# Block linear attention and a gated MLP on one core: the attention state moved ahead, the layer norm split over two engines, and a new order of the instructions

## The chip, the cores and the metric

The kernel runs on one core of a Trainium2 chip. The metric is device microseconds of one execution. Thirteen executions of the kernel before took 151.11 to 153.46 us, median 151.86 us.

## What is computed

q, k and v have the shape (4, 8, 768, 64): batches, heads, positions, channels. Attention is linear with a decay lam per head, and the reference does it in blocks of 64 positions:

```python
for b in range(nb):
    intra = einsum('bhic,bhjc->bhij', qb, kb) * Dmask
    out[:, :, sl] = einsum('bhij,bhjd->bhid', intra, vb) + einsum('bhid,bhde->bhie', qb * lam_pow, kv_state)
    kv_state = lam_block * kv_state + einsum('bhsd,bhse->bhde', kb * rev_pow, vb)
```

The result x (4, 768, 512) goes through a gated MLP. w_in is 512 x 1024, w_spatial 768 x 768, w_out 512 x 512:

```python
h = maximum(x @ w_in, 0.0); u, v = h[..., :512], h[..., 512:]
v_n = (v - mean(v)) / sqrt(var(v) + 1e-06)
v_s = einsum('ts,bsd->btd', w_spatial, v_n) + b_spatial
out = (u * v_s) @ w_out
```

All inputs and the output are float32; the matrix products run in bf16.

## The kernel before, in words

The 4 x 768 positions are cut into 12 tiles n of 256 positions, three for each batch. A tile is worked on in two chunks c of 128 positions. The decay is put into factors of q and v (lq, lqn, lv), so that the recurrence over blocks becomes a running sum: the state of a batch is a sum of k-transposed times v that stays in PSUM bank 7 for the three tiles and is copied to SBUF (s_sb) after each chunk.

**Who sets the order.** Nothing is scheduled by a compiler. A long string ORDER holds one token for each step, and the loop at L501 calls one helper for each token, so that each engine's queue holds its steps in the order of the string. Semaphore waits are put in from what each instruction reads and writes. A token is NAME.arguments.engine; the engines are T (TensorE, PE in the profile), D (VectorE, DVE), A (ScalarE, ACT), P (GpSimd, POOL) and S (SyncE, SP). The first argument is the tile n, or for the MLP's last steps the batch; the last is mostly the PSUM bank.

The steps of a tile, in the order in which data passes through them:

- LK, LQ, LV (`load`, L181): a DMA of 512 KB of k, q or v, asked on SP; three buffers each.
- KC, QC (`split`): a cast to bf16. TK, TQ (L300): eight 128x128 transposes on PE. EK: the copy of the transposed k to SBUF. EQ (L313): the same for q, times lq. For tiles 8 to 11 QM (L277, a product with lqn) and DMA transposes on SP (DK, DQ) take the place of QC, TK, TQ, EK and EQ.
- VD (L292): v times lv, 128 x 1024.
- SC (L329): scores, 16 matmuls of 64x64 tiles. There are two SC for each tile. MK (L333): the scores times the causal mask, on DVE.
- KV (L345): k-transposed times v onto the state in bank 7. SS (L350, a `copy`, L166): the state to SBUF.
- AV (L366 state times q, L375 scores times v): the output products of the attention, in two parts (0 and 1) for the two chunks. Both parts write the same two banks; a 64-row half of the array writes one bank in part 0 and the other in part 1.
- EX: the attention output x-transposed to SBUF.
- PV (L401) and PU (L439): x times the two halves of w_in. EV, EU (L406 on ACT, L408 on DVE): relu and eviction.
- BN (L416, L417): mean and variance on DVE. RA (L421): square root on ACT. RD (L426): reciprocal on DVE. VN (L430): (v - mean) times rstd, 128 x 512, on DVE.

The steps of a batch: PW (L461, six matmuls of 128 x 384) multiplies w_spatial, GB (L466) adds the bias, GM (L472) multiplies by u, PO (L478) multiplies by w_out, EO evicts and ST stores. WT (L451) transposes w_spatial once and EW copies it to SBUF.

The weights are float32 in memory and cast to bf16 by DMAs that GpSimd issues: WI (`w_in`, L239, two halves), WS (`w_sp`, L244, two halves), WO (`w_out`, L248). Ahead of each stands a GT token (`after`, L235), a copy of one element of a q, k or v buffer: it holds POOL's queue until that tile has landed, and so sets when the weights are asked for. GT.1.1 waits for q of tile 1 (0 is k, 1 is q, 2 is v).

The matmuls of the attention (SC, KV, AV) work on 64x64 tiles, four of them in the array at once; all others use the full array.

Of the kernel before, what the change touches and what calls it, by code (L numbers as in the profile page):

```python
# [8 lines left out]
FP32 = mybir.dt.float32  # L9
# [7 lines left out]
LK.0.2.S lam.A msk.P LQ.0.2.S LK.1.2.S idn.P mkc.D LV.0.2.S LB.6.T pos.P LN.6.A LK.2.2.S LL.D KC.0.2.P LX.A  # L17
LQ.1.2.S TK.0.6.T LT.0.A QC.0.2.D LQ.2.2.S TQ.0.5.T EK.0.6.A EQ.0.5.D KC.1.2.A SC.0.0.0.T LV.1.2.S SC.0.1.2.T
LT.2.A MK.0.0.0.D TK.1.6.T VD.0.2.P EK.1.6.A MK.0.1.2.D LV.2.2.S LT.1.A AV.0.0.0.T LK.3.2.S KV.0.0.T SS.0.0.A
GT.1.1.P WI.0.P QC.1.2.D KV.0.1.T AV.0.1.0.T KC.2.2.A LQ.3.2.S GT.1.1.P WI.1.P TQ.1.6.T EX.0.1.1.A TK.2.5.T  # L20
EQ.1.6.D GT.1.2.P WS.1.P EX.0.0.0.A QC.2.2.D EK.2.5.A SC.1.0.2.T LQ.4.2.S GT.1.2.P WS.0.P SC.1.1.0.T
MK.1.0.2.D TQ.2.6.T SS.0.1.A VD.1.2.P EQ.2.6.D MK.1.1.0.D SC.2.0.2.T SC.2.1.4.T MK.2.0.2.D AV.1.0.0.T KV.1.0.T
LV.3.2.S MK.2.1.4.D SS.1.0.A KV.1.1.T VD.2.2.P AV.1.1.0.T SS.1.1.A PV.0.0.6.T EX.1.1.1.A EX.1.0.0.A PV.0.1.1.T
EV.0.0.6.A AV.2.0.2.T BN.0.0.D PV.1.1.6.T EV.0.1.1.D KV.2.0.T BN.0.1.D PV.1.0.5.T SS.2.0.A EV.1.1.6.D RA.0.A
AV.2.1.2.T BN.1.1.D PU.1.0.6.T BS.S EV.1.0.5.A RD.0.D PU.0.1.4.T VN.0.0.D EX.2.1.3.A KC.3.2.P BN.1.0.D
EX.2.0.2.A PU.1.1.5.T EU.0.1.4.A EU.1.0.6.D PV.2.0.3.T RA.1.A VN.0.1.D EU.1.1.5.A RD.1.D TK.3.6.T VN.1.1.D
EV.2.0.3.A PU.2.0.2.T VN.1.0.D EK.3.6.A BN.2.0.D PV.2.1.3.T EU.2.0.2.A PU.2.1.6.T EV.2.1.3.A LK.4.2.S WT.3.2.T
BN.2.1.D EU.2.1.6.A QC.3.2.P WT.4.3.T WT.0.5.T EW.3.2.D RA.2.A WT.1.6.T LK.5.2.S EW.4.3.D EW.0.5.A WT.5.4.T
WT.2.2.T RD.2.D VN.2.1.D EW.5.4.A TQ.3.3.T QC.4.2.P VN.2.0.D PU.0.0.5.T EW.2.2.A EQ.3.3.D LQ.6.2.S EW.1.6.A
TQ.4.4.T VD.3.2.P SC.3.1.0.T EU.0.0.5.A EQ.4.4.D SC.3.0.2.T PW.0.0.1.6.T LQ.5.2.S MK.3.1.0.D PW.0.1.1.5.T  # L30
GB.0.0.1.6.D LV.4.2.S MK.3.0.2.D PW.0.1.0.4.T GM.0.0.1.P KC.4.2.A PW.0.0.0.6.T GB.0.1.1.5.D GB.0.1.0.4.D
LK.6.2.S GM.0.1.1.P TK.4.5.T GB.0.0.0.6.D PW.0.2.1.4.T GM.0.1.0.P EK.4.5.D LK.7.2.S AV.3.0.0.T GT.0.5.P WO.P
GB.0.2.1.4.D SC.4.0.2.T SC.4.1.5.T KV.3.0.T MK.4.0.2.D PW.0.3.1.4.T GM.0.2.1.P SS.3.0.A LV.6.2.S QC.6.2.P
MK.4.1.5.D KV.3.1.T AV.3.1.0.T KC.5.2.A PW.0.3.0.3.T GM.0.0.0.P SS.3.1.D GB.0.3.1.4.D LV.5.2.S QC.5.2.A
TK.5.6.T EX.3.1.1.D GM.0.3.1.P PW.0.2.0.2.T GB.0.3.0.3.D EX.3.0.0.A VD.4.2.P EK.5.6.A GM.0.3.0.D TQ.5.3.T
GB.0.2.0.2.D PV.3.1.5.T EQ.5.3.D PU.3.0.6.T EV.3.1.5.A GM.0.2.0.P AV.4.0.0.T BN.3.1.D EU.3.0.6.A SC.5.1.2.T
SC.5.0.4.T LQ.8.2.S KV.4.0.T MK.5.1.2.D PV.3.0.6.T SS.4.0.A MK.5.0.4.D KV.4.1.T EV.3.0.6.A AV.4.1.0.T LK.8.2.S
KC.6.2.P PO.0.0.3.T EX.4.0.0.A BN.3.0.D EX.4.1.1.A PO.0.1.6.T EO.0.0.3.D RA.3.A LK.9.2.S PV.4.0.2.T RD.3.D
SS.4.1.D EO.0.1.6.A VN.3.1.D VD.6.2.P VN.3.0.D PV.4.1.3.T EV.4.0.2.A ST.0.0.S TK.6.6.T BN.4.0.D EV.4.1.3.A
PO.0.2.2.T EK.6.6.A BN.4.1.D VD.5.2.P TQ.6.3.T LV.9.2.S EO.0.2.2.A PU.3.1.5.T EQ.6.3.D RA.4.A PO.0.3.6.T  # L40
QM.8.0.D QM.8.1.P EU.3.1.5.A ST.0.1.S RD.4.D AV.5.0.0.T VN.4.1.D EO.0.3.6.A SC.6.0.2.T VN.4.0.D SC.6.1.4.T
KV.5.0.T MK.6.0.2.D PO.0.5.6.T SS.5.0.A KC.7.2.P ST.0.3.S AV.5.1.0.T MK.6.1.4.D LQ.11.2.S TK.7.3.T EX.5.1.1.A
PU.4.0.2.T EX.5.0.0.A EK.7.3.A PV.5.1.5.T LK.10.2.S EU.4.0.2.A PV.5.0.4.T ST.0.2.S EV.5.1.5.A LQ.7.2.S
PU.5.1.3.T EO.0.5.6.A BN.5.1.D EV.5.0.4.A PO.0.4.6.T EU.5.1.3.A BN.5.0.D ST.0.5.S PU.5.0.2.T EO.0.4.6.A
LV.8.2.S RA.5.A PU.4.1.3.T EU.5.0.2.A RD.5.D VN.5.0.D AV.6.0.0.T VN.5.1.D EU.4.1.3.A KV.6.0.T ST.0.4.S
PW.1.0.0.6.T SS.6.0.A PW.1.0.1.5.T GB.1.0.0.6.D LQ.9.2.S GM.1.0.0.P PW.1.1.0.6.T GB.1.0.1.5.D LV.7.2.S
QC.7.2.D GM.1.0.1.P KV.6.1.T AV.6.1.0.T GB.1.1.0.6.D KC.8.2.A PW.1.2.0.5.T EX.6.0.0.D DQ.8.S GM.1.1.0.P
EX.6.1.1.A SS.6.1.D PW.1.2.1.6.T DK.8.S GB.1.2.0.5.D VD.8.2.P PW.1.3.0.5.T GB.1.2.1.6.D LK.11.2.S PU.6.0.6.T
GB.1.3.0.5.D GM.1.2.0.P TQ.7.4.T GM.1.3.0.D EU.6.0.6.A GM.1.2.1.P PU.6.1.5.T EQ.7.4.D LV.11.2.S QM.9.0.P
PO.1.0.6.T EU.6.1.5.A SC.7.0.0.T VD.7.2.P EO.1.0.6.A SC.7.1.2.T PO.1.2.5.T MK.7.0.0.D LQ.10.2.S PV.6.1.6.T  # L50
MK.7.1.2.D QM.9.1.P PO.1.1.4.T LV.10.2.S EV.6.1.6.A EO.1.2.5.D AV.7.0.0.T BN.6.1.D EO.1.1.4.A SC.8.1.2.T
SC.8.0.5.T KV.7.0.T MK.8.1.2.D PV.6.0.4.T ST.1.1.S SS.7.0.A KV.7.1.T MK.8.0.5.D EV.6.0.4.A AV.7.1.0.T
# [24 lines left out]
"""


@with_exitstack  # L80
def kernel(
    ctx: ExitStack,
    tc: tile.TileContext,
    q: bass.AP,
    k: bass.AP,
    v: bass.AP,
    lam: bass.AP,
    moe_w_in: bass.AP,
# [6 lines left out]
    P = 128  # L95
# [15 lines left out]
    def sb(shape, dt, name):  # L111
        return const.tile(shape, dt, name=name)
# [18 lines left out]
    lv = sb([P, NR, H, 2], FP32, "lv")  # L131
    lqn = sb([P, NR, H, 2], FP32, "lqn")
    lq = sb([P, NR, 4, 2, P], BF16, "lq")
    seen = sb([1, 1], FP32, "seen")
    eps_t = sb([P, 1], FP32, "eps_t")
    win_sb = sb([P, NCH, DFF], BF16, "win_sb")
    wout_sb = sb([P, NCH, DM], BF16, "wout_sb")
# [397 lines left out]
```

## Time and profile before

| | |
|---|---|
| Median of 13 executions | 151.86 us |
| The profiled execution | 151.52 us |
| Its span, first to last instruction | 149.7 us |
| Mean granted TensorE clock | 0.986 |
| DMA packets' data | 30.73 MB, mean 205 GB/s |

The numbers of the profile are those of the span: between span and device time lie 1.8 us. The profile page gives the busy time of each engine (PE is the matmul stream, PEld the loading of weights beside it), then the span in 40 slices of 3.74 us, where a digit is the busy share in tenths. PEclk is the clock that PE was granted. Further views are the waits (who waited for whom), the chain of work that ended last, the instructions in order of time, and tables of busy time by stretch.

### The profile page before, as it was taken

To read this page: it belongs to the slowest core of one execution; us is meant where nothing else is said; L and a number is where in the kernel's file an instruction comes from. 1 tells how busy PE (TensorE), PEld (TensorE's weight loads), DVE (VectorE), ACT (ScalarE), POOL (GpSimd) and SP (SyncE) were. 2 spreads that over 40 slices of the span, in tenths; PEclk is the share of its full clock that TensorE was granted. 3 is DMA by queue.
4 is the path that set the end of the run, shared out by engine and by line. 5 is a ranking of instruction groups with operands and counts; after the bars stand their busy time and mean duration, and the time that the engine had idled before them with its cause. 6 is when DMAs were issued, how large, how long until landed. Compare 5 with 4: busy or idle time off the path is not lost.

```text
span 149.7 us, 4756 instructions
## 1 busy us (share of the span) xinstructions
PE 135.0 (90%) x2026; PEld 88.0 (59%) x2026; DVE 106.3 (71%) x190; ACT 81.3 (54%) x146; POOL 75.2 (50%) x74
## 2 busy tenths in 40 slices
PE   1274959999999989999999999999999999999990
PEld 1263845487866754667766657557667655666540
DVE  1445492985798999994567799999949981936701
ACT  3987815398921836849812445676552245831161
POOL 7415990203739966740049967980393340016620
PEclk9999995999999999999999999999999999999998
DMA  3999999999999999999999799997170003111165
GB/s 98 299 290 290 290 216 217 216 236 309 286 278 253 217 293 283 294 309 279 333 336 198 177 307 316 107 209 262 30 120 4 2 4 140 70 70 72 70 227 198
DMA packets 52040, 30.73 MB, mean 205 GB/s; under 512 B 9522, under 2 KB 48946, under 8 KB 52018
## 3 DMA queue, kind: packets, MB, share of 16 engines
q1 hardware_dynamic: 49488, 27.53, 73.9%
q0 software_dynamic: 2384, 2.75, 10.8%
q8 instruction: 16, 0.26, 0.7%
q10 hardware_dynamic: 146, 0.13, 0.3%
q14 instruction: 6, 0.05, 0.1%
HBM read 24.77 MB, written 6.29 MB: 207 GB/s over the span
## 4 chain that ended last, share of the span: by engine, by line
PE 82%; DVE 4%; issue 2%; ACT 1%; ACTq 0%
PE ps L461 20%; PE ps L401 14%; PE ps L478 14%; PE ps L439 14%; PE ps L375 4%; PE ps L345 4%; PE ps L300 4%; PE ps L329 3%; PE ps L366 3%; DVE a_sb L333 2%; PE ps L451 1%; DVE vsb L466 1%; DVE qT L313 0%; DVE gT L472 0%; DVE o_sb L170 0%
## 5 line engine op out<-in xcount | busy, mean ns | idle before, releaser
L472 POOL TENSOR_TENSOR gT<-vsb,uT 128x384 bf16<-128x384 f32 x27 | 30.1, 1130 | 33.5 <-DVE vsb L466 33.3
L461 PE MATMUL ps<-wt_sb,vn 128*128 128x384 bf16 x192 | 33.9, 327 | 0.0
L292 POOL TENSOR_TENSOR vd<-v_in,lv 128x1024 bf16<-128x1024 f32 x12 | 22.9, 1910 | 14.4 <-issue 6.4
L333 DVE TENSOR_TENSOR a_sb<-ps,m 128x1024 bf16<-128x1024 f32 x24 | 28.4, 1214 | 1.8 <-PE ps L329 1.6
L416 DVE BATCH_NORM_STATS2 st<-vh 128x6 f32<-128x512 bf16 x24 | 16.5, 686 | 11.9 <-ACT vh L406 11.7
L461 PEld LDWEIGHTS <-vn 128*128 128x128 bf16 x192 | 17.9, 98 | 11.9
L401 PE MATMUL ps<-win_sb,xT 128*128 128x512 bf16 x96 | 24.6, 393 | 0.0
L439 PE MATMUL ps<-xT,win_sb 128*128 128x256 bf16 x192 | 24.1, 273 | 0.0
L478 PE MATMUL ps<-wout_sb,gT 128*128 128x512 bf16 x96 | 23.4, 380 | 0.0
L466 DVE TENSOR_TENSOR vsb<-ps,bsp 128x384 f32<-128x384 f32 x32 | 17.6, 552 | 6.8 <-PE ps L461 5.4
L439 PEld LDWEIGHTS <-win_sb 128*128 128x128 bf16 x192 | 18.3, 98 | 4.4
L168 ACT ACTIVATE o_sb<-ps 128x512 f32<-128x512 f32 (+1 forms) x21 | 12.4, 589 | 14.4 <-PE ps L478 10.2
L406 ACT ACTIVATE vh<-ps 128x512 bf16<-128x512 f32 x21 | 12.6, 601 | 13.5 <-PE ps L401 13.5
L406 ACT ACTIVATE uT<-ps 128x512 bf16<-128x512 f32 x22 | 13.2, 598 | 6.3 <-PE ps L439 6.1
L401 PEld LDWEIGHTS <-xT 128*128 128x128 bf16 x96 | 9.0, 101 | 9.7 <-issue 1.5
L168 ACT ACTIVATE s_sb<-ps 128x256 bf16<-128x256 f32 x14 | 5.3, 381 | 16.9 <-PE ps L345 16.9
L478 PEld LDWEIGHTS <-gT 128*128 128x128 bf16 x96 | 9.0, 98 | 8.9
L430 DVE TENSOR_SCALAR vn<-vh,mv,rstd 128x512 bf16<-128x512 bf16 x24 | 12.3, 546 | 0.3
L375 PE MATMUL ps<-a_sb,vd 64*64 64x128 bf16 x384 | 11.2, 229 | 1.1 <-DVE a_sb L333 1.1
L168 ACT ACTIVATE kc<-k_in 128x1024 bf16<-128x1024 f32 x7 | 7.4, 1056 | 7.3 <-PE ps L345 5.1
L168 ACT ACTIVATE xT<-ps 128x512 bf16<-128x512 f32 x19 | 10.5, 592 | 1.3 <-PE ps L375 1.1
L329 PE MATMUL ps<-qT,kT 64*64 64x128 bf16 x384 | 8.5, 233 | 2.3 <-DVE qT L313 2.3
(64 smaller groups left out, 156.4 us busy)
## 6 DMA issues: line engine op xcount, KB each, us to landing
k_in<-in_k_dram SPq DMA_DIRECT2D x12, 512.0 KB, 7.1
q_in<-in_q_dram SPq DMA_DIRECT2D x12, 512.0 KB, 7.4
v_in<-in_v_dram SPq DMA_DIRECT2D x12, 512.0 KB, 8.1
out_dram<-o_sb SPq DMA_DIRECT2D x23, 256.0 KB, 2.8
wsp_raw<-in_moe_w_spatial_dram POOLq DMA_DIRECT2D x2, 576.0 KB, 15.7
win_sb<-in_moe_w_in_dram POOLq DMA_DIRECT2D x2, 512.0 KB, 10.2
wout_sb<-in_moe_w_out_dram POOLq DMA_DIRECT2D x1, 512.0 KB, 8.5
bsp<-in_moe_b_spatial_dram SPq DMA_DIRECT2D x1, 384.0 KB, 8.3
```

The costliest lines, as they stand in the source:

```text
L168: nc.scalar.activation(out=o, in_=i, func=AF.Copy)
L292: vec(e).tensor_tensor(out=vd[n % NCA][:, h], in0=v_in[n % NIN][:, h], in1=lv[:, n % NR, h].unsqueeze(3).broadcast_to((P, h.stop - h.start ...
L333: nc.vector.tensor_tensor(out=a_sb[n % NA][:, i].rearrange("p o w j x -> p (o w) (j x)"), in0=bank(b, 2).rearrange("p o (w y) -> p (o w) y ...
L375: nc.tensor.matmul(out=po[row(w), c ^ o, c, i], lhsT=vd[n % NCA][row(c), 4 * o + u, j, :], rhs=a[row(c), i, o, w, j, :], start=(r == 0 and ...
L401: nc.tensor.matmul(out=bank(b), lhsT=x[:, c, g], rhs=win_sb[:, g, DH:DFF], start=(g == 0), stop=(g == NCH - 1))
L406: nc.scalar.activation(out=o, in_=i, func=AF.Relu)
L416: nc.vector.bn_stats(out=st6[p2][:, t], in_=vh[p2][:, t])
L439: nc.tensor.matmul(out=pu[:, f2].rearrange("p (c x) -> p c x", c=2), lhsT=win_sb[:, g, f * P:(f + 1) * P], rhs=x[:, :, g, :], start=(g == ...
L461: nc.tensor.matmul(out=bank(b)[:, 0:HW], lhsT=vn[bb % 2][:, s, f * P:(f + 1) * P], rhs=wt_sb[:, s, i * HW:(i + 1) * HW], start=(s == 0), s ...
L466: nc.vector.tensor_tensor(out=vsb[(bb * 4 + f) % NVS][:, i * HW:(i + 1) * HW], in0=bank(b)[:, 0:HW], in1=bsp[:, i * HW:(i + 1) * HW], op=A ...
L472: vec(e).tensor_tensor(out=gT[bb % 2][:, f, cols].rearrange("p (a y m) -> p a y m", m=2, y=Q64), in0=vsb[(bb * 4 + f) % NVS][:, cols].rear ...
L478: nc.tensor.matmul(out=bank(b), lhsT=gT[bb % 2][:, f, t * P:(t + 1) * P], rhs=wout_sb[:, f, :], start=(f == 0), stop=(f == NCH - 1))
```

## The change

The diff consists of a new ORDER and four small edits.

- State ahead: KV of the next chunk or tile now stands ahead of AV where it can (KV.1 before AV.1 is as before; KV.5.0 and KV.6.0 now stand before AV.5.0 and AV.5.1), and KV, AV and the SC of the next tile stand in one row on PE.
- Between the two parts of an AV of the tiles 3 to 11 there is a new step SY: a copy of one element of each of the two banks (ps[0:1, b:b+2, 0:1]) into `seen`, five times on ACT and four times on DVE. Part 1 writes the banks that SY reads, and SY reads what part 0 wrote, so that part 1 starts when part 0 is done.
- VN has a second form on ACT: Identity with scale rstd and bias nmr = -mean times rstd. Sixteen of the 24 VN are there. RD has one more DVE instruction, which makes nmr (128 x 2).
- The weights are asked elsewhere: WI.0 after v of tile 0, WI.1 after v of tile 1, WS.1 after k of tile 2, WS.0 after v of tile 2, WO after v of tile 5. Before: all of WI after q of tile 1, WS after q of tile 2, WO after k of tile 5.
- SP asks q, k, v of the tiles 0 to 2 as K0 Q0 V0 K1 Q1 V1 Q2 K2 V2; before as K0 Q0 K1 V0 K2 Q1 Q2 V1 V2.
- Other steps change engine: 9 instead of 3 EV, 4 instead of 2 EU and 8 instead of 5 GM are on DVE, one VD (VD.1) is on DVE, EK.0 and others go from ACT to DVE, some QC from DVE and ACT to POOL.

The work on PE is the same: 194 steps, 4051 instructions.

```diff
 ORDER = """
-LK.0.2.S lam.A msk.P LQ.0.2.S LK.1.2.S idn.P mkc.D LV.0.2.S LB.6.T pos.P LN.6.A LK.2.2.S LL.D KC.0.2.P LX.A
-LQ.1.2.S TK.0.6.T LT.0.A QC.0.2.D LQ.2.2.S TQ.0.5.T EK.0.6.A EQ.0.5.D KC.1.2.A SC.0.0.0.T LV.1.2.S SC.0.1.2.T
-LT.2.A MK.0.0.0.D TK.1.6.T VD.0.2.P EK.1.6.A MK.0.1.2.D LV.2.2.S LT.1.A AV.0.0.0.T LK.3.2.S KV.0.0.T SS.0.0.A
-GT.1.1.P WI.0.P QC.1.2.D KV.0.1.T AV.0.1.0.T KC.2.2.A LQ.3.2.S GT.1.1.P WI.1.P TQ.1.6.T EX.0.1.1.A TK.2.5.T
...
+LK.0.2.S lam.A idn.P LQ.0.2.S msk.P LV.0.2.S LK.1.2.S LB.6.T pos.P mkc.D LN.6.A LQ.1.2.S LL.D KC.0.2.P LX.A
+LV.1.2.S TK.0.6.T LT.0.A QC.0.2.D EK.0.6.D TQ.0.5.T LT.1.A LQ.2.2.S EQ.0.5.D GT.2.0.P WI.0.P LT.2.A SC.0.0.0.T
+LK.2.2.S SC.0.1.2.T VD.0.2.P MK.0.0.0.D KC.1.2.A MK.0.1.2.D LV.2.2.S TK.1.6.T AV.0.0.0.T QC.1.2.D EK.1.6.A
+KV.0.0.T TQ.1.5.T SS.0.0.D AV.0.1.0.T EQ.1.5.D KV.0.1.T EX.0.0.0.A SS.0.1.D SC.1.1.2.T SC.1.0.4.T EX.0.1.1.A
+MK.1.1.2.D LK.3.2.S MK.1.0.4.D GT.2.1.P WI.1.P PV.0.1.6.T VD.1.2.D LQ.3.2.S PV.0.0.5.T EV.0.1.6.A QC.2.2.P
+AV.1.0.0.T BN.0.1.D EV.0.0.5.A LQ.4.2.S KV.1.0.T BN.0.0.D TQ.2.6.T SS.1.0.A GT.0.2.P WS.1.P KC.2.2.A
+AV.1.1.0.T EQ.2.6.D KV.1.1.T EX.1.0.0.D SS.1.1.A TK.2.6.T EX.1.1.1.A RA.0.A PV.1.1.5.T EK.2.6.D SC.2.1.0.T
+SC.2.0.2.T EV.1.1.5.A PV.1.0.6.T MK.2.1.0.D BS.S PU.0.0.5.T RD.0.D EV.1.0.6.A BN.1.1.D GT.2.2.P WS.0.P
+VN.0.1.A PU.0.1.4.T BN.1.0.D EU.0.0.5.A VD.2.2.P PU.1.0.6.T VN.0.0.A MK.2.0.2.D EU.0.1.4.A PU.1.1.5.T RA.1.A
+EU.1.0.6.A RD.1.D VN.1.1.D AV.2.0.0.T VN.1.0.A LV.3.2.S EU.1.1.5.A KV.2.0.T SS.2.0.A KC.3.2.D AV.2.1.0.T
+EX.2.0.0.D EX.2.1.1.A TK.3.6.T PV.2.1.5.T EK.3.6.A PV.2.0.4.T EV.2.1.5.A PU.2.0.6.T BN.2.1.D EV.2.0.4.A
+LK.4.2.S WT.1.5.T BN.2.0.D EU.2.0.6.A WT.5.4.T QC.3.2.P EW.1.5.A WT.4.3.T EW.5.4.D WT.0.6.T WT.3.2.T RA.2.A
...
+SC.5.0.4.T SY.4.0.D LQ.9.2.S KV.4.1.T MK.5.1.2.D AV.4.1.0.T SS.4.1.A PV.3.1.6.T EX.4.0.0.A VD.6.2.P MK.5.0.4.D
+EX.4.1.1.A TQ.6.0.T LV.7.2.S PU.4.1.1.T EV.3.1.6.D QC.7.2.P PU.4.0.5.T EQ.6.0.D EU.4.1.1.A LV.9.2.S BN.3.1.D
+PV.4.1.6.T GT.2.5.P WO.P EU.4.0.5.D KC.6.2.A PW.0.2.1.4.T VD.5.2.P EV.4.1.6.D LK.8.2.S TK.6.5.T BN.4.1.D
+PV.3.0.6.T EK.6.5.A GB.0.2.1.4.D KV.5.0.T LV.8.2.S EV.3.0.6.D AV.5.0.0.T GM.0.2.1.P SS.5.0.A SC.6.1.2.T
+SC.6.0.4.T SY.5.0.D BN.3.0.D KV.6.0.T AV.5.1.0.T KC.7.2.P PV.4.0.6.T EX.5.0.0.A MK.6.0.4.D EX.5.1.1.A TK.7.0.T
...
-    seen = sb([1, 1], FP32, "seen")
+    seen = sb([1, 2], FP32, "seen")
...
+    nmr = many(2, [P, NT], FP32, "nmr")
...
-        nc.gpsimd.tensor_copy(out=seen, in_=(k_in, q_in, v_in)[x][n % NIN][0:1, 0, 0, 0:1])
+        nc.gpsimd.tensor_copy(out=seen[:, 0:1], in_=(k_in, q_in, v_in)[x][n % NIN][0:1, 0, 0, 0:1])
...
+    def s_y(e, n, b):
+        copy(e, seen, ps[0:1, b:b + 2, 0:1].rearrange("p z x -> p (z x)"))
...
     def r_d(e, n):
         r, p2 = n % NR, n // NR % 2
-        nc.vector.reciprocal(out=rstd[p2][:, 2 * r:2 * r + 2], in_=rstd[p2][:, 2 * r:2 * r + 2])
+        pair = slice(2 * r, 2 * r + 2)
+        nc.vector.reciprocal(out=rstd[p2][:, pair], in_=rstd[p2][:, pair])
+        nc.vector.scalar_tensor_tensor(out=nmr[p2][:, pair], in0=mv[p2][:, pair, 0], scalar=-1.0,
+                                       in1=rstd[p2][:, pair], op0=ALU.mult, op1=ALU.mult)
 
     def v_n(e, n, c):
         t, p2 = 2 * (n % NR) + c, n // NR % 2
+        if e == "A":
+            nc.scalar.activation(out=vn[p2][:, t], in_=vh[p2][:, t], func=AF.Identity,
+                                 scale=rstd[p2][:, t:t + 1], bias=nmr[p2][:, t:t + 1])
+            return
```

## The prediction

> **What bounds the kernel now.** I read the page's busy shares and slices first, then the busy time by stretch, then the PE's waits, then the chain, last the DMA queues around the weights.
>
> ```profile
> PE 135.0 (90%) x2026; PEld 88.0 (59%) x2026; DVE 106.3 (71%) x190; ACT 81.3 (54%) x146; POOL 75.2 (50%) x74
> ...
> PE   1274959999999989999999999999999999999990
> ...
> PEclk9999995999999999999999999999999999999998
> DMA  3999999999999999999999799997170003111165
> ```
>
> PE is full from the seventh slice (3.74 us each) to the last but one; it idles in the first 22 us, and in slice 7 its clock is halved. DMA is full until about 100 us.
>
> ```profile
> 22.50:36.50 14.00, 13.94 (x176) 8.75 (x175) 8.85 (x21) 9.33 (x18) 2.09 (x3) 0.88 1.17 240
> 36.50:146.10 109.60, 108.87 (x1593) 69.00 (x1592) 85.25 (x151) 56.46 (x101) 58.41 (x48) 1.00 0.79 193
> ```
>
> From 36.5 to 146.1 us (columns: length, then busy of PE, PEld, DVE, ACT, POOL, clock, DMA, GB/s) PE idles 0.73 us. So **PE's own work bounds the kernel**; only three things can be won: the start, PE time between matmuls that counts as busy, and those 0.73 us. The last 3.6 us (146.1 to 149.7: eviction and store) end with the same instructions in both kernels.
>
> ```profile
> PE ps L300 <- POOL kc L172: 2.6, 1, 2.6
> PE ps L329 <- DVE qT L313: 2.3, 3, 0.9
> PE ps L345 <- ACT s_sb L168: 1.3, 2, 0.9
> PE ps L375 <- DVE a_sb L333: 1.1, 1, 1.1
> ```
>
> After 6.1 us PE waits 5.6 us in all (the 2.6 us lie before that), 4.9 of them before 22.6 us. One stall stands later:
>
> ```profile
> 55.27 0.64 PE L329 MATMUL ps<-qT,kT 64*64 64x128 bf16 x32 [0.70 <-DVE qT L313]
> ```
>
> **Mode switches.** The chain's pieces (start, us, what) show PE time that is neither waiting nor work:
>
> ```profile
> 40.60 0.57 PE ps L329 x32
> ...
> 45.63 0.98 PE ps L461 x6
> 46.60 0.35 PE ps L375 x16
> 46.95 0.45 PE ps L329 x32
> 47.40 0.24 PE ps L345 x16
> 47.64 1.08 PE ps L461 x6
> ```
>
> 32 score matmuls (64x64 tiles) take 0.57 right after full-array transposes and 0.45 after other 64x64 work; six W_spatial matmuls (128x128) take 1.08 after 64x64 work and 0.98 after full-array work. A switch between 64x64 and full-array work costs 0.10 to 0.12, I take 0.11. Counting them in the PE order: up to the first WT 14 before and 14 after; from there on 42 before, 28 after, since SC, KV and AV now stand together ("KV.5.0 AV.5.0 SC SC KV.6.0 AV.5.1"). 14 x 0.11 = **-1.54 us**. It counts only where PE is full, as it is there; otherwise it is worth 0.
>
> **The stall at 55.27.** TQ.5 ended 2.4 us of PE work ahead of SC.5, but its qT multiply stood on DVE behind a gT product of 2.68 (L472) and an addition. Now TQ.5, PU, PU, KV, AV, SC.5: again 2.4 us, and on DVE only MK.4 stands ahead of the multiply (0.69), done by then: **-0.70**. What is late next there is counted below as new misses.
>
> **The start, step by step.** Both orders hold the same PE work before the first WT, which starts here:
>
> ```profile
> 36.53 2.20 PE L451 MATMUL ps<-ident,wsp_raw 128*64 128x128 bf16 x72
> ```
>
> So the lead of the new start is 36.5 minus its WT start. Tiles of q, k, v (512 KB) land 1.81 us apart (kc waits until 5.0, qc 6.8, kc.1 8.6, vd 10.5). The new order asks K0 Q0 V0 K1 Q1 V1 Q2 K2 V2, so V0 lands at 8.6 (was 10.5), K1 at 10.4 (was 8.6), Q1 at 12.2 (was 14.0). W_in's first half is asked when V0 is there instead of Q1. It comes through POOL's queue:
>
> ```profile
> 14.69 0.93 POOL L239 DMA_DIRECT2D win_sb<-in_moe_w_in_dram  x1
> ```
>
> Its first packets run in the 18 to 19 us stretch, some 3.7 us later, and the landing views give W_in 8.9 and 11.5 us from issue, W_spatial 14.3 and 17.1 (queued behind W_in). While POOL's transfers run, the others starve (20 to 22 us: packets, MB, share):
>
> ```profile
> q0 software_dynamic: 290, 0.29, 84.3%
> q1 hardware_dynamic: 282, 0.14, 34.9%
> ```
>
> Packets alternate one to one, and POOL's are the larger: q, k, v fall from 0.29 MB/us to 0.07. Worked on with these rates: the copy after V0 0.7, W_in half 0 issued at 9.3, flowing at 13.0, landed by 18.1; V1 lands at 15.2, Q2 18.5; W_in half 1 issued at 15.4, landed by 24.3 (26.9 with the other row); K2 at 22.1 (was about 12), W_spatial.1 issued at 22.3; V2 at 25.0, W_spatial.0 issued at 25.2, flowing behind .1, landed at **34.6** - as before (17.5 + 17.1 = 34.6).
>
> [...]
>
> PE, with the durations of its first 24 us: TK.0 6.1, TQ.0 7.5, SC.0 9.4 to 10.5 as before. K1's cast now stands behind all three LT on ACT (to 10.55), so TK.1 starts at 11.7 (was 10.4), AV.0.0 at 12.7 (12.5), KV.0.0, TQ.1 13.8 to 14.8, AV.0.1 and KV.0.1 to 16.0, SC.1 to 17.1. Then PE waits 1.0 for W_in and runs two PV (1.73, or 2.89 at half clock) that before came at 23.8. VD.1 is now on DVE behind two MK (19.1 + 1.4 = 20.5; 1.36 from two 128x512 products of L277, 1.91 from POOL), so AV.1.0 starts at 20.6; TQ.2, AV.1.1, KV.1.1 to 22.7, TK.2 waits for K2's cast to 23.2; PV.1.1 at 24.3, SC.2, PV.1.0 to 26.8, four PU to 30.3, AV.2, KV.2, a wait of 0.5 for the state copy, AV.2.1 to 32.0, TK.3, two PV, PU: **WT at 35.3**, a lead of 1.2. If the clock halves once, as here,
>
> ```profile
> 19.03:22.44 3.41, 1.78 (x77) 1.45 (x76) 3.39 (x5) 0.32 (x1) 3.06 (x2) 1.00 1.20 217
> 22.44:25.86 3.42, 3.30 (x45) 1.77 (x45) 1.08 (x1) 1.70 (x5) 0.07 (x1) 0.51 1.19 216
> ```
>
> (3.4 us with PE half busy are followed by 3.4 us at 0.51), TK.2 and PV.1.1 end about 0.8 later: lead 0.4. I take the middle, **-0.8**; bounds +0.5 (W_in half 1 and V1 both late) and -1.9 (WT can't start before 34.6).
>
> [...]
>
> **What is added.** Nine SY copies (two elements from PSUM), 5 on ACT, 4 on DVE. No row has one; 0.06 (memset 128x1) to 0.41 (128x256 from PSUM), nearest 0.18 (ACT 128x8 from PSUM, L202). PE's second AV part waits for it: 0.04 + 0.18 + 0.06 = 0.3 after the first part. Behind that wait stand all of PE's later matmuls. Cover between: for n = 4, 5, 6, 8, 9, 10 two SC and one KV (0.45 + 0.24 = 0.69), for 3, 7, 11 over 1.7. Taken at 0; without cover 0.3 each. Sixteen VN go from DVE (0.55 mean, 0.41 median) to ACT (0.60 by L406's 128x512; at least 0.30, the small sqrt); twelve 128x2 products are added on DVE (0.16 to 0.18). The same three table loads stay on ACT. With the other moves DVE carries by these rows about 3 us more and ACT 4 more, of 43 and 68 us idle: hidden behind PE; uncovered, a late VN holds up a PW on PE for as long as it is late.
>
> **New misses.** On POOL, VD.6 (1.9) waits for AV.4.1 (at 53.3), then QC.7 (1.04), the copy, the W_out issue (0.8), VD.5 (1.9): 59.2, and PE wants KV.5.0 at about 59.6; KC.7 and W_out (8.5 from issue: 65, wanted at 66) follow as tightly. Between 0 and 2.0; I take +0.4.
>
> **Sum.** Profiled execution 151.52 (span 149.7 and 1.8 around it): -0.8 - 1.54 - 0.70 + 0.40 = -2.64, 148.9. It lies 0.34 under the median of 151.86, so **149.2**.
>
> **Rivals.**
> - The start is worth all it can be: 151.86 - 1.9 - 1.54 - 0.70 = 147.7, lower if W_spatial lands early (146.8). For: WI.0 lands 5.5 us earlier. Against: K2, K1's cast and VD.1 come later. 0.15.
> - No change: no lead, POOL's chain slips 2.0: 151.86 - 1.54 - 0.70 + 2.0 = 151.6. For: margins of 0.4 there. 0.16.
> - Slower: **W_spatial lands late.** Its second half is asked at V2's landing (25.2) instead of 17.5. WT wants it at 35.7; 17.1 us as before would make 42.3, 6.6 late: 155.8; 8.5 (W_out's row) hides it. It turns the sign from a landing after 39.1, 13.9 us from issue. Against: only its own other half is ahead of it. 0.13.
> - The SY wait is bare: with two evictions (0.6 each) ahead of the copy it ends 1.5 after the first part, 0.8 uncovered, six times: 154.0; sign turns at 0.57 each. 0.06.
>
> **Chances.** The forecast, 147.9 to 151.0: 0.50. About 0.5% (0.76 us) is what a measurement tells from no change; so faster 0.65, same 0.16, slower 0.19. Range 146.8 to 152.9: it leaves out most of the slower cases and the edge of the fast one.
>
> **What would show it.** In the new profile: WT's first matmul at 34.6 to 36.1; PE idle after it under 1.2 us; half clock in one slice or none; no PE wait over 0.3 on "seen"; pieces of L461 x6 with 1.08 rarer. Wrong if WT waits for DMA, if SY shows as a releaser, or if PE idles after 40 us on POOL's vd.

## The result, and the profile after

The changed kernel took 153.8 us (median of 11 executions, 152.7 to 154.19); the kernel before, on the same chip, 152.4 us. The ratio is **1.0133, 95% interval 1.0105 to 1.016: slower by 1.3%**, where 1.8% faster was forecast. Single executions of the kernel before lie in two groups, about 151.5 and 153, and the ratios leave out a kernel's executions that are over 1.5% above its fastest, so the table below also gives the ratio of the medians over all executions (1.009 here).

The profiled execution took 154.19 us (before 151.52), its span is 152.5 us. The page, busy shares and slices (3.81 us each):

```profile
PE 135.0 (89%) x2026; PEld 87.6 (57%) x2026; DVE 109.8 (72%) x200; ACT 85.9 (56%) x158; POOL 71.9 (47%) x73
...
PE   1259598959999899999999999999999999999980
...
PEclk9999999996999999999999999999999999999998
DMA  3999999999999985999799999655674010151055
```

PE's busy time is what it was, 135.0. Its gaps, before in the fourth and sixth slices, are now in the fifth and in the ninth (5, at 30 to 34 us); in the tenth the clock falls (6). The stretches, divided at the first WT (39.58, before 36.53):

```profile
22.50:39.55 17.05, 14.63 (x228) 9.36 (x222) 10.79 (x21) 12.46 (x22) 4.82 (x6) 0.90 1.14 269
39.55:148.25 108.70, 107.67 (x1593) 69.19 (x1592) 85.42 (x158) 60.60 (x113) 57.40 (x48) 1.00 0.72 183
```

From the first WT to the last matmul it is 108.6 us (109.5 before); the start is 3.05 longer; the last eviction and store take 4.3 instead of 3.7 us (3.6 to 4.2 in the other kernels below). -0.9 + 3.05 + 0.6 = 2.8: **in this execution the start loses more than the whole.** It is the slowest of the eleven; the medians lie 1.4 us apart, not 2.8. PE's waits, in us, times, longest:

```profile
PE ps L406 <- DMA win_sb<-in_moe_w_in_dram: 1.9, 1, 1.9
...
PE ps L368 <- ACT s_sb L170: 1.4, 1, 1.4
...
PE ps L473 <- DVE vsb L478: 0.6, 1, 0.6
```

The state copy (s_sb), which the order moved ahead, is itself what PE waits for. PE's instructions around it, in order of time:

```profile
33.98 0.31 PE L368 MATMUL ps<-qT,s_sb 64*64 64x128 bf16 x8 [1.43 <-ACT s_sb L170]
...
35.19 3.50 PE L406 MATMUL ps<-win_sb,xT 128*128 128x512 bf16 x8
...
39.58 0.58 PE L463 MATMUL ps<-ident,wsp_raw 128*64 128x128 bf16 x14
```

AV.2.1 waits 1.43, and then the PV.2 pair (8 matmuls) takes 3.50, nearly twice its time in the profiles below where the clock stays (1.90). ACT's instructions show why the copy is late:

```profile
29.20 0.81 ACT L439 ACTIVATE vn<-vh,nmr,rstd 128x512 bf16<-128x512 bf16 x1 [0.82 <-DVE nmr L433]
29.92 0.57 ACT L411 ACTIVATE uT<-ps 128x512 bf16<-128x512 f32 x1
30.40 0.80 ACT L439 ACTIVATE vn<-vh,nmr,rstd 128x512 bf16<-128x512 bf16 x1
...
32.35 0.81 ACT L439 ACTIVATE vn<-vh,nmr,rstd 128x512 bf16<-128x512 bf16 x1
...
33.55 0.37 ACT L170 ACTIVATE s_sb<-ps 128x256 bf16<-128x256 f32 x1
```

Its state was complete at 32.5 (KV.2.0 ran from 32.10, 0.44). Three VN, needed by nobody before 44 us, stand ahead of it, and the first of them made ACT wait 0.82 for nmr. That product of 128x2 elements took 0.16 in eight of its twelve places, and 1.09 here, first row; the second is POOL's VD.2 beside it:

```profile
28.01 1.09 DVE L433 SCALAR_TENSOR_TENSOR nmr<-mv,rstd 128x2 f32<-128x2 f32 x1
```
```profile
27.16 1.91 POOL L294 TENSOR_TENSOR vd<-v_in,lv 128x1024 bf16<-128x1024 f32 x1
```

They end at 29.10 and 29.07. The nmr is not needed for the delay: in the run sy_four below, whose order is the same up to here, ACT did not wait for it and the copy ran at 33.55 all the same. The clock, by stretches (columns as above, the clock is the third from the end):

```profile
31.70:35.10 3.40, 1.86 (x72) 1.36 (x63) 1.90 (x6) 2.78 (x7) 0.00 (x0) 1.00 1.14 249
35.10:38.50 3.40, 3.31 (x9) 1.20 (x10) 0.99 (x3) 1.61 (x3) 0.00 (x0) 0.53 1.14 320
```

A stretch in which PE was 55% busy is followed by one at 0.53. It is the pattern that the kernel before shows once, at 19.03 to 25.86; there the first PV pair took 2.96 (23.77). Here the first pair ran slowly too (18.58, 3.40 us), but at a recorded clock of 1.00: PE's matmuls had been as slow before it (28 of SC.1 took 1.04 at 15.66; 32 of SC.2 took 0.64 at 26.14), so that no wait is shown to be the reason.

Nor does the second halving belong to the order. The run h2_rest_before below has the same order up to here, the same wait and nearly the same busy time, and its clock stays:

```profile
33.98 0.31 PE L366 MATMUL ps<-qT,s_sb 64*64 64x128 bf16 x8 [1.44 <-ACT s_sb L168]
...
35.20 1.90 PE L404 MATMUL ps<-win_sb,xT 128*128 128x512 bf16 x8
```
```profile
31.70:35.10 3.40, 1.89 (x72) 1.40 (x64) 1.89 (x6) 2.78 (x6) 0.00 (x0) 1.00 1.13 253
```

So does that of sy_four (wait 1.24 at 33.97, pair 1.90, first WT at 37.90). Of the 3.05 us that the start loses in the profile, about 1.6 are this halving, which came in one of three profiles with this wait; 1.4 are there without it.

### The profile page after: what moved, and what is told of

Its sections match the earlier page's. It is cut to its first block, busy times and chain, and to the rows that moved or that the text cites. A ratio compares the mean times of both kernels' runs of the same rounds, so it can differ in the third digit from the quotient of the medians.

```text
span 152.5 us, 4771 instructions
## 1 busy us (share of the span) xinstructions
PE 135.0 (89%) x2026; PEld 87.6 (57%) x2026; DVE 109.8 (72%) x200; ACT 85.9 (56%) x158; POOL 71.9 (47%) x73
## 4 chain that ended last, share of the span: by engine, by line
PE 64%; DVE 10%; DMA 8%; ACT 7%; SPq 6%; issue 2%; ACTq 0%; DVEq 0%
PE ps L473 20%; PE ps L406 12%; PE ps L451 11%; PE ps L490 10%; DMA k_in<-in_k_dram 8%; SPq L186 6%; DVE a_sb L335 3%; PE ps L377 2%; PE ps L331 2%; ACT vn L439 2%; DVE nmr L433 2%; PE ps L302 2%; PE ps L347 2%; DVE vsb L478 2%; PE ps L368 2%
## 5 line engine op out<-in xcount | busy, mean ns | idle before, releaser
L484 POOL TENSOR_TENSOR gT<-vsb,uT 128x384 bf16<-128x384 f32 x24 | 26.1, 1105 | 42.7 <-DVE vsb L478 41.6
L406 PE MATMUL ps<-win_sb,xT 128*128 128x512 bf16 x96 | 26.8, 419 | 2.2 <-DMA win_sb<-in_moe_w_in_dram 1.9
L294 POOL TENSOR_TENSOR vd<-v_in,lv 128x1024 bf16<-128x1024 f32 x11 | 21.0, 1905 | 10.6 <-PE ps L451 9.3
L490 PE MATMUL ps<-wout_sb,gT 128*128 128x512 bf16 x96 | 22.4, 379 | 0.0
L439 ACT ACTIVATE vn<-vh,nmr,rstd 128x512 bf16<-128x512 bf16 x16 | 12.8, 812 | 5.7 <-DVE nmr L433 5.7
L411 ACT ACTIVATE vh<-ps 128x512 bf16<-128x512 f32 x15 | 8.9, 592 | 12.7 <-PE ps L406 11.7
L170 ACT ACTIVATE xT<-ps 128x512 bf16<-128x512 f32 x21 | 11.6, 592 | 7.7 <-PE ps L377 7.7
L411 ACT ACTIVATE uT<-ps 128x512 bf16<-128x512 f32 x20 | 11.7, 590 | 5.5 <-PE ps L451 5.5
L302 PE MATMUL ps<-ident,kc 128*128 128x128 bf16 x64 | 5.8, 243 | 5.0 <-POOL kc L174 3.6
L279 POOL TENSOR_TENSOR qc<-q_in,lqn 128x512 bf16<-128x512 f32 x7 | 7.7, 1116 | 3.3 <-issue 3.3
```

The source lines that it names most:

```text
L170: nc.scalar.activation(out=o, in_=i, func=AF.Copy)
L294: vec(e).tensor_tensor(out=vd[n % NCA][:, h], in0=v_in[n % NIN][:, h], in1=lv[:, n % NR, h].unsqueeze(3).broadcast_to((P, h.stop - h.start ...
L406: nc.tensor.matmul(out=bank(b), lhsT=x[:, c, g], rhs=win_sb[:, g, DH:DFF], start=(g == 0), stop=(g == NCH - 1))
L411: nc.scalar.activation(out=o, in_=i, func=AF.Relu)
L439: nc.scalar.activation(out=vn[p2][:, t], in_=vh[p2][:, t], func=AF.Identity, scale=rstd[p2][:, t:t + 1], bias=nmr[p2][:, t:t + 1])
L484: vec(e).tensor_tensor(out=gT[bb % 2][:, f, cols].rearrange("p (a y m) -> p a y m", m=2, y=Q64), in0=vsb[(bb * 4 + f) % NVS][:, cols].rear ...
```

## The experiments

**Theory A**: the loss lies in the start, made by ACT's queue (the three VN and the nmr ahead of the state copy) and by the halved clock that the wait brings. Its second half is not borne out, as the lines of h2_rest_before above show. **Rival B**: the start is late by its transfers, K2 above all. Further rivals are named in the expectations. The table has, from each profiled execution, the start of the first WT and the time from there to the last matmul; then the ratio to the kernel before on the same chip, and that of the medians over all executions.

| kernel | first WT | WT to last | ratio, 95% interval | medians |
|---|---|---|---|---|
| before | 36.53 | 109.5 | | |
| after | 39.58 | 108.6 | 1.0133 (1.0105 to 1.016) | 1.009 |
| h1_start_before | 38.63 | 110.6 | 1.0218 (1.0162 to 1.0274) | 1.016 |
| h2_rest_before | 39.62 | 112.6 | 1.0433 (1.0369 to 1.0498) | 1.037 |
| ss_dve | 36.50 | 109.1 | 1.0031 (0.9983 to 1.0079) | 0.999 |
| warm | 37.80 | 110.1 | 1.0117 (1.0073 to 1.0161) | 1.005 |
| vn_dve | 36.85 | 110.3 | 1.0088 (1.0039 to 1.0137) | 1.000 |
| k2_early | 41.49 | 108.7 | 1.0221 (1.0107 to 1.0335) | 1.018 |
| sy_four | 37.9 | 114.6 | 1.0432 (1.0354 to 1.0509) | 1.034 |
| before_warm | 36.2 | 111.2 | 1.0033 (0.9977 to 1.0089) | 0.996 |
| start_dve | 36.89 | 109.1 | 0.9904 (0.9869 to 0.9938) | 0.993 |
| start_dve_warm | 36.35 | 108.9 | 0.9953 (0.9899 to 1.0007) | 0.996 |
| ss_warm | 38.76 | 109.4 | 0.9895 (0.9851 to 0.994) | 0.993 |
| before_warm2 | 36.77 | 110.1 | 0.9973 (0.994 to 1.0006) | 0.999 |
| vn_behind_ss | 37.56 | 110.1 | 1.0017 (0.9984 to 1.0051) | 1.001 |
| vn3_dve | 37.78 | 110.3 | 0.9899 (0.9811 to 0.9987) | 0.995 |
| before_vn_act | 38.29 | 111.6 | 1.0227 (1.0132 to 1.0321) | 1.017 |

**The two halves exchanged.** The order up to the first WT from one kernel, the rest from the other. At the seam both have one PU ahead of the first WT that the rest's own kernel has behind it (1.0 us of PE), so their WT is 1.0 later and their rest 1.0 shorter than for the same work. In h1 a WT also writes bank 6 before EU.2.1 has read it, so that this part of u is written over.

> The order of before up to the first WT, the new order from there on (with SY, the second form of VN and the new engines). Theory A (the new start loses 3 us and the rest gains 1): WT starts at 36.5 as before, the stretch from WT to the last matmul takes 108.5 to 109, and the time is 0.5 to 1.2 us below before. Rival C (the rest of the new order, SY among it, is what costs): the time is 1 us or more above before.

> The new order up to the first WT, the order of before from there on (no SY, VN of tiles 3 to 11 on DVE). Theory A: WT starts at 38 to 39.6 and the time is 2 to 3 us above before, more than the new kernel itself. Rival C: within 0.7 us of before.

Both are slower than either kernel. The rest that took 108.6 after its own start took 110.6 after the other one (PE waits 2.8 us in it instead of 0.8), and the old rest 112.6 instead of 109.5. Theory A's numbers fell, for h1 in sign and for h2 in size (over 5 us for 2 to 3): each rest is fitted to what its own start leaves landed and free, and halves can't be priced by exchange.

**The state copy on DVE.**

```diff
-SS.2.0.A
+SS.2.0.D
```

> The new kernel with one step moved: the state copy SS.2.0 goes from ACT, where it stands behind VN.1.0 and two EU, to DVE. Theory A: PE's wait of 1.43 us before AV.2.1 falls to 0.5, the two PV after it no longer run at half clock, and WT starts 0.9 us (clock still halved) to 2.6 us (not halved) earlier; the time falls by as much. Rival B (k of tile 2 and the weights come too late and hold the whole start): WT does not move by more than 0.3 us.

PE's wait before AV.2.1 is 0.52, the PV.2 pair runs in 1.90 (which h2_rest_before had without the change), and the first WT comes 3.1 earlier; 1.4 of these were there already at TK.2, since W_in landed sooner in this execution (first PV pair at 17.12 instead of 18.58). The nmr product took 2.01 here beside the same POOL product (26.62 to 28.63; POOL 26.69 to 28.60), and PE waited 1.09 for a uT behind VN and nmr. By the ratio, one changed token takes most of the loss away.

**Fillers against the clock.**

```diff
+DM.18.6.T        (18 matmuls ident x ident, 128x128, into bank 6)
 AV.2.1.0.T
```

> The new kernel with 18 matmuls of the identity (128 columns, 1.0 us at full clock) into the free bank 6 ahead of AV.2.1, where PE waits 1.43 us; they are added work, and nothing reads them. Theory A with the clock as its second part: PE still goes on at 34.0, but the two PV at 35.2 take 1.73 instead of 3.5 us, and WT starts 1.7 us earlier; the time falls by 1.7. If the halved clock does not come from the wait (or costs nothing, because something later is waited for): no change of the time, or 0.1 more.

The PV.2 pair takes 1.90 and the WT comes 1.8 earlier, the numbers that theory A gave. But sy_four has the same pair and a WT at 37.90 without fillers, so this run does not show what they do. And 1.0 is given back: TQ.4 waits that long for the cast of q of tile 4, which stands on DVE behind the nmr of tile 2, beside a POOL product:

```profile
39.83 1.63 DVE L436 SCALAR_TENSOR_TENSOR nmr<-mv,rstd 128x2 f32<-128x2 f32 x1
```
```profile
39.55 1.90 POOL L293 TENSOR_TENSOR vd<-v_in,lv 128x1024 bf16<-128x1024 f32 x1 [7.90 <-DMA v_in<-in_v_dram]
```
```profile
42.45 0.62 PE L301 MATMUL ps<-ident,qc 128*128 128x128 bf16 x8 [1.02 <-DVE qc L171]
```

The nmr and POOL's product end at 41.46 and 41.45. The ratio hardly moves: behind a WT that comes 1.8 earlier, a long nmr stood beside a POOL product at another place.

**All layer norm back on DVE**, nmr left out.

```diff
-VN.0.1.A ... (16 times)
+VN.0.1.D ...
```

> The new kernel with all 24 VN on DVE as before, at their new places in the order, and without the 12 products that make nmr. Theory A (ACT's queue, fed by DVE's nmr product that took 1.09 us, delays the state copy SS.2.0): the four PU run without the wait for uT, SS.2.0 is no longer behind two VN of 0.81 us, but three VN of 0.41 go to DVE ahead of MK.2.0; WT 0.5 to 1.5 us earlier, and the time falls by 0.5 to 2 us. If the layer norm on ACT is no part of the loss: within 0.5 us of the new kernel or slower.

The first WT comes 2.7 earlier and the column shows no halved clock (mean 1.00; the first PV pair took 3.32 even so), but the rest takes 1.6 more: PE waits 1.32 for a_sb at 76.5 and 0.57 for vsb at 95.9, both behind VN on DVE. So the sixteen VN on ACT are a loss in the start and a gain later.

**K2 asked earlier (rival B).**

```diff
-LV.1.2.S ... LK.2.2.S ... GT.2.1.P WI.1.P ... GT.0.2.P WS.1.P
+LK.2.2.S ... LV.1.2.S ... GT.0.2.P WI.1.P ... GT.2.1.P WS.1.P
```

> The new kernel with k of tile 2 asked and the weights' second request released one place earlier: SP asks K0 Q0 V0 K1 Q1 K2 Q2 V1 V2, W_in's second half is asked when K2 lands and W_spatial's first when V1 lands. Rival B (the chain of the new kernel begins with K2's transfer of 12.9 us, so its landing sets the start): TK.2 at 23.0 instead of 24.4, WT 1 us or more earlier. Theory A: K2's cast stands on ACT behind SS.1.0, which is done at 23.1 in any case, so TK.2 moves by 0.2 and WT by less than 0.4 us.

V1 came later by it; PE waited 1.82 for the vd of tile 1, and WT came at 41.49. PE's matmuls also stayed slow until about 31 us (8 transposes took 1.04 at 27.51, at a column of 1.00), so the run prices neither K2 nor V1. What holds against rival B is the changed kernel's own row: PE waits 0.47 for K2's cast (24.41), which bounds what an earlier K2 alone can win at that place.

**SY made four times as long**, to see its cover.

> The new kernel with each SY made of four copies of 0.14 to 0.16 us in place of one. Theory A and the prediction (SY is covered by 0.69 us of PE work or more): four copies take 0.04 + 0.6 + 0.06 = 0.70, so PE waits at most 0.1 at each of six places; within 0.6 us of the new kernel. Rival C in the form that the SY wait costs: each of the nine waits grows by 0.45, and the time by 4 us.

One SY takes 0.14 to 0.16 and no wait of PE stands on it in the changed kernel. Four of them bring 0.8 of waits on DVE's and 0.5 on ACT's copies, but the rest is 6.0 us longer: both numbers expected, 0.6 and 4, were too small. Of the other 4.7 us, 1.1 is the wait at TQ.4 that warm has too; later waits and 1.7 us more of busy PE make up the rest, and are not explained. So four copies cost far more than the waits on them, and the run does not tell how much cover one has to spare.

**Fillers in the kernel before.** In the first version the fillers ahead of AV.1.0 write over scores in bank 5 that were still to be masked, and those ahead of KV.1.1 wait 1.49 for that masking; the second uses bank 6 for both.

> The kernel before with 27 matmuls of the identity (128 columns) into the free bank 5 in three gaps in which PE waits (ahead of SC.2.0, AV.1.0 and KV.1.1, 19 to 22.6 us); nothing reads them. If the halved clock comes from those gaps: the two PV at 23.8 take 1.8 instead of 2.9 us, WT starts at 35.2 to 35.5, and the time falls by 0.7 to 1.3 us. If not, or if the transfers hold WT: no change.

> The kernel before with 27 fillers in its own start, where PE waits up to 22 us (12 ahead of SC.2.0, 8 ahead of AV.1.0, 7 ahead of KV.1.1; the results are not used, and they write only banks that are free). Theory A, of the clock: no halved stretch at 22.4 to 25.9 us, WT at 35.0 to 36.0 (36.53 without them). If the gain is kept the ratio is 0.988 to 0.998; if the rest gives it back, as the fillers in the changed kernel saw 1.0 us given back at a transposition of q, waits after WT are over 1.5 us and the ratio is 0.998 to 1.006.

In both the first PV pair took 1.9 instead of 2.96: the clock was not halved (mean granted clock 0.998 and 0.999, one profile each). But in the second the pair started 0.45 later, 0.33 of it a wait for W_in, and PE paused 0.63 at 27.13 for a reason the profile does not name; WT at 36.77, missed. These fillers did not make the old start faster.

**The queue relieved: four steps of the start on DVE**, no nmr for the tiles 0 and 1.

```diff
-VN.0.1.A VN.0.0.A VN.1.0.A SS.2.0.A
+VN.0.1.D VN.0.0.D VN.1.0.D SS.2.0.D
...
         nc.vector.reciprocal(out=rstd[p2][:, pair], in_=rstd[p2][:, pair])
+        if n < 2:
+            return
```

> The changed kernel with four steps of the start put on DVE: the layer norm of tile 0 (both chunks) and of tile 1 (chunk 0), and the state copy of tile 2, chunk 0; tiles 0 and 1 need no nmr then, so its two products are left out there. The other 13 layer-norm steps stay on ACT. Theory A (the start loses its time in ACT's queue at 28 to 34 us, where three VN of 0.81 and an nmr of 1.09 stand ahead of the state copy, and in the halved clock that the wait brings): no PE wait over 0.6 before AV.2.1, the PV.2 pair at 1.9 us, WT at 36.0 to 37.3, first WT to last matmul 108.3 to 109.3 as in the changed kernel, ratio to the kernel before 0.993 to 1.004. Rival C (the start is late because of its transfers, and the earlier WT with the state copy on DVE or all VN on DVE came from an early landing of W_in): WT at 38.5 or later, ratio over 1.008.

Faster than the kernel before by 1.0% (over all ten executions 151.46 against 152.49, 0.7%; four of the ten lie at 153.0 to 153.9): it beats both kernels. PE's instructions, to be laid beside those of the changed kernel:

```profile
32.97 0.31 PE L367 MATMUL ps<-qT,s_sb 64*64 64x128 bf16 x8 [0.52 <-DVE s_sb L171]
...
34.19 1.90 PE L405 MATMUL ps<-win_sb,xT 128*128 128x512 bf16 x8
...
36.89 0.30 PE L464 MATMUL ps<-ident,wsp_raw 128*64 128x128 bf16 x4
```

TK.2 started even 0.4 later than in the changed kernel (24.82, W_in landed as late), so the transfers did not help. AV.2.1 starts 1.01 earlier, the pair takes 1.60 less, and that makes 2.6 of the 2.69 that the first WT gains. Only the 1.01 is put down to the change: against sy_four, whose clock stayed, the WT is 1.0 earlier. The stretch ahead of the pair now has PE busy for 2.81 of 3.40 us, and the clock stays:

```profile
31.70:35.10 3.40, 2.81 (x77) 1.88 (x74) 2.47 (x7) 1.99 (x3) 0.00 (x0) 1.00 1.13 249
35.10:38.50 3.40, 3.40 (x71) 2.65 (x71) 2.41 (x6) 2.86 (x7) 0.00 (x0) 1.00 1.14 319
```

Rival C (only early landings made such starts fast) is refuted.

**The same with fillers**: 14 ahead of the first PV pair and 8 ahead of AV.2.1, once with the four steps on DVE, once with the state copy alone.

> As start_dve, and 22 filler matmuls (128x128, into a free bank, their result is not used): 14 ahead of the first PV pair, 8 ahead of AV.2.1, so that PE is busy while it waits. Theory A (a halved clock at the first PV pair, 3.40 instead of 1.73 us, is the other part of the loss): the pair takes under 2.2 us, WT at 34.6 to 36.0, ratio 0.985 to 0.998. Rival D (what the start gains is given back where q and k of the tiles 3 and 4 have not landed, at 40 to 46 us): WT as above, but waits of 0.8 us or more between 40 and 46 us, first WT to last matmul over 109.6, ratio 0.998 to 1.006.

> The changed kernel with only the state copy of tile 2, chunk 0, on DVE, and the same 22 fillers. Against start_dve_warm it tells what the three VN on ACT cost. Theory A: the wait of PE for uT behind VN and nmr (1.09 us with the copy alone moved) stays at 0.5 to 1.1 us, WT 0.5 to 1.2 us later than in start_dve_warm, ratio 0.992 to 1.004. Rival C: WT within 0.3 us of start_dve_warm, the VN cost nothing.

In the first the wait for W_in is gone and the WT comes 0.5 earlier, but TK.2 now waits 1.28 for k of tile 2; the ratio is no better. In the second the profiled execution was its slowest (153.53 of 150.21 to 153.53), in which k of tile 2 landed late (PE waits 2.68 at 25.35), so its WT does not tell the VN's price. Between these three the timed ratios decide nothing.

**What in the queue costs: order, work, or the split itself.** First only the order in ACT's queue, then only the three VN, then the split alone in the kernel before.

```diff
-VN.0.0.A ... VN.1.0.A ... SS.2.0.A           (vn_behind_ss)
+SS.2.0.A VN.0.0.A VN.1.0.A
-VN.0.1.A VN.0.0.A VN.1.0.A                   (vn3_dve; no nmr for n < 2)
+VN.0.1.D VN.0.0.D VN.1.0.D
```

> The changed kernel with two tokens moved and nothing else: VN.0.0 and VN.1.0, on ACT as before, now stand behind the state copy of tile 2, chunk 0, in ACT's queue instead of ahead of it. Theory A1 (the order in the queue costs, not the work): the state copy runs at 32.2 to 32.7 us instead of 33.55, PE's wait for s_sb is 0.3 to 0.6 instead of 1.43, the PV.2 pair runs at 1.9, WT at 36.8 to 37.8, ratio 0.990 to 1.003. Rival A2 (the work on ACT costs, wherever it stands): the wait moves to the next copies of ACT (xT, kT), WT over 38.3, ratio 1.006 or more.

> The changed kernel with only the three layer-norm steps of the start (tile 0 both chunks, tile 1 chunk 0) on DVE, their nmr left out; the state copy stays on ACT. Theory A1: as vn_behind_ss, WT at 36.5 to 37.8, ratio 0.988 to 1.003. If the state copy's own engine matters (ACT's queue is late even without the three), WT is over 38 and the ratio over 1.004.

> The kernel before with the split alone: the same 16 layer-norm steps on ACT, each at its old place in the order, and the 12 nmr products on DVE. Its ACT queue holds the state copy of tile 2 ahead of all of them. Theory A1: the start does not suffer, WT at 36.3 to 36.9, and 16 steps of 0.81 hide behind PE: ratio 0.997 to 1.006. Rival A2: they delay evictions on ACT everywhere, PE waits over 2 us more, ratio over 1.010.

*vn_behind_ss*: ACT and then PE,

```profile
32.53 0.38 ACT L169 ACTIVATE s_sb<-ps 128x256 bf16<-128x256 f32 x1 [0.37 <-PE ps L346]
32.81 1.51 ACT L438 ACTIVATE vn<-vh,nmr,rstd 128x512 bf16<-128x512 bf16 x2
34.22 0.58 ACT L169 ACTIVATE xT<-ps 128x512 bf16<-128x512 f32 x1
```
```profile
32.97 0.31 PE L367 MATMUL ps<-qT,s_sb 64*64 64x128 bf16 x8 [0.47 <-ACT s_sb L169]
34.86 1.90 PE L405 MATMUL ps<-win_sb,xT 128*128 128x512 bf16 x8 [0.81 <-ACT xT L169]
42.41 0.62 PE L301 MATMUL ps<-ident,qc 128*128 128x128 bf16 x8 [1.23 <-DVE qc L171]
```

The wait for the state falls from 1.43 to 0.47 by order alone (A1). Then the next copy in the queue, xT, is late by 0.81 (the half of A2 that holds), and TQ.4 gives back 1.23: a VN on DVE ahead of its cast took 2.08, beside the POOL product that stood beside the nmr in warm. The ratio goes from 1.013 to 1.002 (medians: 1.009 to 1.001).

*vn3_dve*: with the state copy left on ACT its wait is 0.47 too. The ratio of 0.990 rests on two of four executions; all four give 0.995, near start_dve's 0.993 (the profiled one is its slowest). The three VN ahead of the copy, with the nmr that this run leaves out too, are the cause of its delay. Either side can be moved: ss_dve, which moves the copy, shortens that wait as much.

*before_vn_act*: rival A2 holds, A1 is refuted. PE's waits in it that the kernel before does not have:

```profile
37.32 1.03 PE L446 MATMUL ps<-xT,win_sb 128*128 128x256 bf16 x8 [0.59 <-ACT kT L168]
...
43.22 0.42 PE L329 MATMUL ps<-qT,kT 64*64 64x128 bf16 x16 [0.51 <-ACT wt_sb L168]
...
100.16 1.90 PE L401 MATMUL ps<-win_sb,xT 128*128 128x512 bf16 x8 [0.49 <-ACT xT L168]
```

Each is a copy on ACT behind a VN. The split alone costs 2.3% in the old order (medians: 1.7%). Of the 2.1 us that its rest takes longer, 1.2 are waits; the other 0.9 stay open.

## Why the prediction was wrong, by its steps

- **PE's own work bounds the kernel: right.** After the first WT PE waits 0.70 us before and 0.79 after.
- **Mode switches (-1.54): right in sign, too large.** Without its waits PE needs 108.83 us from the first WT before and 107.85 after: -0.98 for 14 fewer switches, 0.07 each where 0.11 was taken. That the switches are all of it is argued, not shown.
- **The stall (-0.70): gone, and replaced.** Nothing waits at SC.5; but PE waits 0.60 at 49.98 for vsb and 0.19 at 75.54 for s_sb. The "new misses" of +0.4 were expected from POOL's vd; no wait on vd came, the miss came from the bias additions on DVE. Together -0.30 was forecast, +0.09 measured.
- **The start (-0.8): the step that failed; measured +3.05.** The forecast WT of 35.3 was missed by 4.3. W_in came at 18.58 instead of 18.1: 0.5. The first PV pair held PE for 3.33, to the start of the next step, instead of 1.73: 1.6. The wait for the state copy was 1.43 instead of 0.5: 0.9. The second pair held it for 3.29 instead of 1.73: 1.6. Together 4.6, of which 0.3 came back elsewhere. Without the second pair's 1.6, which h2_rest_before and sy_four do not have, WT is at 37.9 (sy_four): still 1.4 later than before, where a lead of 0.8 was forecast. The transfers had been worked out nearly right (W_in within 0.5; k of tile 2 cast in time for a TK.2 at 24.41, forecast 23.2).
- **What lay behind it** is the sentence that called the VN "hidden behind PE" and let a late VN hold up only a PW. Its price was added as ACT's time over the whole span (68 us idle), and ACT's queue at 28 to 34 us was never walked. VN took 0.81 (0.60 was taken, from an eviction out of PSUM), nmr 1.09 in the one place that mattered (0.16). A late VN first held up what stood behind it on ACT. How the late start, and the wait at TQ.4 that four runs with a WT at 37.6 to 37.9 have, add up to the 1.3% in the executions that were only timed is not shown.
- **The clock.** The prediction read from one row that a half-busy stretch halves it, and took a middle between one halving and none. The column shows one, behind a wait that the walk missed; the first pair was as slow at a column of 1.00. It did not come each time: four executions of the changed kernel with a mean granted clock of 1.00 took 153.3 to 153.8 us, so the loss is there without it. PE was busy for 1.86 of 3.40 us ahead of the halved stretch, but the busy share does not decide it: no halving followed 1.89 of the same stretch in h2_rest_before, nor 2.81 in start_dve. What decides stays open.
- **SY: right.** No PE wait stands on it; 0.14 to 0.16 measured, 0.18 taken.
- **The rivals**: none was it. W_spatial landed 8.6 and 9.7 us after it was asked, in time; SY was covered. That the order of one engine's queue in the start could cost more than all three gains was not among them. Of what was to show it, PE's idle time after the WT (0.79, under 1.2) and SY held; the WT at 34.6 to 36.1 did not.

## What to carry to other kernels

Work that is moved to a half-idle engine is priced in that engine's queue at the place where it is put: look at what stands behind it and who waits for that. The same sixteen instructions cost 2.3% in one order; in the other the first three of them cost more than the rest gain (none on ACT 1.009, all sixteen 1.013, without the three 0.990; by the medians 1.000, 1.009, 0.995). A wait of 1.2 to 1.4 us was followed by a PV pair 1.6 slower, at a clock of 0.53, in one profile and by none in two others with the same order and place, so one profile's clock is not put down to an edit before a second profile shows it. A rest of an order is fitted to its start, so test a part by moving it alone, not by joining halves.

## What the runs showed that was not expected

- A DVE product of 128x2 elements (nmr) took 0.16 in eight places of the changed kernel, six of them with no POOL instruction beside it, and 1.09, 0.76, 0.83 and 0.49 beside products and casts of POOL, ending each time within 0.05 us of POOL's instruction; 2.01 in ss_dve, and 1.63, 1.66 and 1.69 for tile 2 in warm, vn3_dve and sy_four, where TQ.4 waited 1.0 to 1.1 behind it. The prediction took 0.16 to 0.18 and did not ask what POOL does beside it. Why the two end together is not shown.
- Each stretch that the clock column shows at half is 3.4 us long, in the nine profiles that have one (22.5 to 25.9 us at 0.51 in the kernel before, 35.3 to 38.7 at 0.50 in the changed one). The column reads 1.00 before it even where matmuls are slow: in the kernel before 8 transposes take 1.04 at 15.62 and 0.62 at 38.66.
- How late k of tile 2 lands differs from profile to profile at the same order of requests: PE waited for its cast 0.47 us in the changed kernel, 0.16 in ss_dve, 0.75 in start_dve, 1.99 in vn3_dve and 2.68 in ss_warm. Why stays open.
